# A prefix-sum mask, V without copies and a new order in the opening of an attention + FFN kernel

## The chip, the cores and the metric

The kernel runs on one core of a Trainium2 chip. The metric is the device time of one execution in microseconds; lower is better. The kernel before takes 326.36 us, the median of three runs (326.13 to 328.28).

## The reference

Causal attention in a sliding window of 64 keys over 8 batches of 8 heads, 576 tokens of 64 dimensions each, and behind it a gated FFN over all 4608 tokens. Inputs and output are float32.

```python
B, H, S, D = 8, 8, 576, 64
scores = (1.0 / np.sqrt(D)) * np.matmul(q, k.transpose(0, 1, 3, 2))
rel = pos[:, None] - pos[None, :]
scores = np.where((rel >= 0) & (rel < 64), scores, -1e9)
attn = softmax(scores)                      # over the keys
x = np.matmul(attn, v)                      # to (4608, 512), heads side by side
g = x @ w_gate                              # 512 x 1536
out = (g * sigmoid(g) * (x @ w_val)) @ w_out   # 1536 x 512
```

## The kernel before

**Tiling.** The 4608 tokens are cut into 36 chunks of 128 and 9 FFN chunks of 512. A query sees at most 64 keys back, so a chunk of 128 queries needs its own 128 keys and the last 64 of the chunk before. Matmuls take bfloat16 and accumulate in float32 in the eight PSUM banks.

**One chunk of attention.** `Sa`, `Sbias` and `Sb` make the scores of chunk n, keys on the partitions, queries along the columns. A score tile has 128 rows for 192 keys: rows 0 to 63 hold the chunk's lower 64 keys, against all 128 queries; rows 64 to 127 hold the 64 keys of the chunk before for the lower 64 queries, and the chunk's own upper 64 keys for the upper 64 queries. In the first four chunks the mask is a matmul that adds `nmask` (0 or -30000) to the bank ahead of the scores (`Sbias`, L459); later chunks multiply the exponentials by `mask` (`Sm`). ScalarE takes the exponential into `pt` (L491). The product with V has a 65th column of ones, so that each result carries its denominator; VectorE divides (`AVn`, L628 and L631) into `xb`. `X` transposes `xb` on PE (L743), and ScalarE or VectorE copies the result into `xT`.

**V in the first chunks.** Queries of the lower half need the own lower keys on partitions 0 to 63 and the keys of the chunk before on partitions 64 to 127. `shift` therefore copies halves of `va` into `vs` on POOL or ScalarE (L298, L296), and `AVs` multiplies per head once by `vs` for the lower 64 queries and once by `va` for the upper 64, each over 128 partitions (L612). Chunk 0 has no chunk before it and takes `va` alone (L609).

**The opening.** `build` writes the order of the first four chunks out by hand, with the PSUM banks in two written lists (`banks`). Each engine works through its own instructions in order, and an instruction waits by semaphore for what it reads and overwrites. k of the first 256 tokens comes through SP's and ACT's DMA queues (`first_loads`). All else comes through POOL's queue: `load2` for q and k in pairs of chunks, `load` for v, `load_w` for pieces of the gate and value weights. POOL also makes `ident` and two steps of the mask with `affine_select` (`init_ident` L320, `init_mask` L329) in the same sequence. PE runs matmuls on zeros (`warm`, L789) while k arrives and in some gaps. `Fs` makes a step of the FFN: a Wg group, then a Wv group (L818), tanh on ScalarE (L825), two products on VectorE (L827, L829). It is a generator, so `build` can place other work between its groups.

**Behind the opening.** `EARLY`, `LOADS` and `SHIPS` list the further steps, and `pump` issues loads as soon as the step that frees their buffer is recorded. At most 16 of POOL's DMAs are outstanding, since it uses 16 semaphores in turn. A bank is then picked by when the recorder's cost model has it free.

Of the kernel before, what the change touches and what calls it, by code (L numbers as in the profile page):

```python
# [7 lines left out]
ALU = mybir.AluOpType  # L8
# [12 lines left out]
F32 = dt.float32  # L21
# [145 lines left out]
class _Kernel:  # L167
# [41 lines left out]
    def alloc(self):  # L209
        nc = self.nc  # L210

        def sb(name, n, dtype=BF):
            return nc.alloc_sbuf_tensor(name, [128, n], dtype)
# [4 lines left out]
        self.ident = sb("ident", 128)  # L218
# [84 lines left out]
    def init(self):  # L303
        g = self.g
        self.zero(self.wup[:, :], ["wup"])
        g.op("act", lambda e: e.activation(self.wup[:, :], self.wup[:, :], ACTF.Exp), writes=["wup"])
        self.zero(self.wz[:, :], ["wz"])
        self.zero(self.ident[:, :], ["ident"])
        self.zero(self.mask[:, :], ["mask"], 1.0)
        self.init_va(0, 4)  # L310
        for i in range(3):
            self.zero(self.vs[i][:, :, 64:80], [("vs", i, 0), ("vs", i, 1)], 1.0)
# [9 lines left out]
            pattern=[[-1, 128]], channel_multiplier=1), writes=["ident"])  # L322

    def init_mask(self):
        g = self.g
        mm = self.mask[:, :].rearrange("p (v e q) -> p v e q", v=3, e=2)
        a, b = mm[:, :, 0, :], mm[:, :, 1, :]
        for fill, base in ((0.0, 0), (1.0, 64)):
            g.op("pool", lambda e, fill=fill, base=base: e.affine_select(  # L329
                out=a, in_=a, compare_op=ALU.is_ge, fill=fill, base=base,  # L330
                pattern=[[0, 3], [1, 64]], channel_multiplier=-1), writes=["mask"])
        src = mm[:, 0:1, 0, :].to_broadcast([128, 3, 64])
        one = g.op("dve", lambda e: e.tensor_scalar(b, src, -1.0, 1.0, ALU.mult, ALU.add), reads=["mask"], writes=["mask"])
        g.op("dve", lambda e: e.memset(mm[64:128, 1, 0, :], 0.0), writes=["mask"])
        g.op("dve", lambda e: e.memset(mm[0:64, 2, 1, :], 0.0), writes=["mask"], after=one)

    def init_nmask(self):
        self.g.op("dve", lambda e: e.tensor_scalar(
            self.nmask[:, :], self.mask[:, :], 1.0, 30000.0, ALU.subtract, ALU.mult), reads=["mask"], writes=["nmask"])

    def init_kmask(self):
        g = self.g
# [255 lines left out]
    def AVs(self, st):  # L598
        n, bx, av, done = st
        va, pt = self.va[n], self.pt[n % self.NP]  # L600
        iv = self.VS[n]
        vs = self.vs[iv] if n else va

        def pe(e):
            for j in range(4):
                for p in range(2):
                    h = 2 * j + p
                    if n == 0:
                        x = e.matmul(av[:, p, j, :], pt[:, h, :], va[:, h, 0:65], start=j == 0, stop=True, skip_group_check=True)  # L609
                        continue  # L610
                    for c, vv in ((0, vs), (1, va)):
                        x = e.matmul(av[64 * c:64 * c + 64, p, j, :], pt[:, h, 64 * c:64 * c + 64], vv[:, h, 0:65],  # L612
                                     start=j == 0, stop=True, skip_group_check=True)
# [6 lines left out]
        done.append(self.g.op("pe", pe, reads=rd, writes=[b[1] for b in bx]))  # L620

    def AVn(self, st):
        n, bx, av, _ = st
# [277 lines left out]
    def loads(self):  # L901
        self.first_loads()
        self.load2(0, "q")
        self.load2(1, "k")
        self.init()
        self.init_ident()
        self.first_cast("k", 0, "dve")
        self.init_mask()
        self.load2(1, "q")
        self.load(0, "v")  # L910
        self.load(1, "v")
        self.load(2, "v")
        self.load(3, "v")
        self.load_w("g", 0, 2)
        self.load_w("v", 0, 2)
        self.load_w("g", 2, 4)
# [5 lines left out]
        self.W(4, 6)  # L922
        self.W(6, 8)

    def ready(self, t):

# [70 lines left out]
    def main(self, t):  # L997
        w = t[0]
        if w == "F":
            c, f = t[1:].split(".")  # L1000
            h = f[-1] if f[-1] in "ab" else ""
# [16 lines left out]
        elif w in "kq":  # L1018
            n = int(t[1:-1])
# [7 lines left out]
        elif w == "A":  # L1027
            n = int(t[1:])
# [3 lines left out]
        elif w == "N":  # L1032
            n = int(t[1:])
            self.AVn(self.held[n])
            self.did.add("a%d" % n)
        elif w == "B":
            n = int(t[1:])
            self.need("v%d" % n, "v%d" % (n - 1), "s%d" % n)
            st = self.AVa(n)
# [6 lines left out]
        elif w == "P":  # L1046
            n = int(t[1:])
            self.need(*["v%d" % m for m in (n - 1, n, n + 1)], "s%d" % n, "s%d" % (n + 1))
            bx = self.two("a") + [self.bank("a")]
# [8 lines left out]
        elif w == "X":  # L1058
            n, e = t[1:].split("/")
            n = int(n)  # L1060
            self.need("a%d" % n)
            self.X(n, e.rstrip("+"), half="+" in e)
            self.did.add("x%d" % n)
        elif w == "H":
            h, e = t[1:].split("/")
            n, r, i = map(int, h.split("."))
            self.need("v%d" % n, "V")
            self.shift(n, r, e, i)
            self.did.add("h" + h)
        elif w == "D":  # L1070
            self.store()
        elif w == "V":
            self.init_va(4, self.NV)
        elif w == "K":
            self.init_kmask()
        self.did.add(t)
# [30 lines left out]
    def build(self):  # L1107
        F, S, AV, X, T2, O = self.F, self.S, self.AV, self.X, self.T2, self.O
        self.loads()
        self.banks("a", [0, 1, 2, 3, 4, 5, 6, 7, 0, 1, 4, 5, 2, 3, 0, 1, 6, 7, 4, 5, 2, 3, 0, 1, 6, 7, 2, 3])  # L1110
# [33 lines left out]
        self.AVs(a2)  # L1144
        self.AVn(a2)
        a3 = self.AVa(3)
        self.AVs(a3)
# [12 lines left out]
        next(f2, None)  # L1160
        next(f1)
        next(f1, None)
        for n in range(4):
# [54 lines left out]
```

## Time and profile before

| | before |
|---|---|
| median of three runs | 326.36 us (326.13 to 328.28) |
| profiled execution | 325.66 us |
| its span, first to last instruction | 323.9 us |
| PE / VectorE / ScalarE / POOL busy | 97 / 63 / 42 / 34% |
| first FFN matmul starts at | 15.92 us |

The profile is of one execution. The span runs from the first instruction to the last; the rest of the execution's time lies around it. A row of the timeline has a start, a length, the engine, the line in the kernel, the operation, the tile written and those read, and the count where several follow one another; in square brackets stands how long the engine had idled and what ended that. The chain of waits follows the work that ended last back to what released it, step by step.

### The profile page before, as it was taken

How to read it: one execution, taken by the hardware profiler on the slowest of the kernel's cores; microseconds unless marked ns; L12 is line 12 of the kernel's file. 1: busy time of each engine (PE TensorE's matmuls, PEld its weight loads, DVE VectorE, ACT ScalarE, POOL GpSimd, SP SyncE). 2: the span in 40 equal slices, each digit the busy share in tenths (PEclk: the TensorE clock that was granted, in tenths of full speed). 3: DMA queues.
4: the chain of work that ended last, by engine and by line, in shares of the span. 5: the costliest groups of instructions: out<-in, count | busy, mean ns of one | idle time of the engine just before them, and what ended most of it. 6: DMA issues, size and time to landing. Idle time of an engine off the chain costs nothing.

```text
span 323.9 us, 7964 instructions
## 1 busy us (share of the span) xinstructions
PE 315.4 (97%) x3395; PEld 170.3 (53%) x3430; DVE 204.1 (63%) x355; ACT 136.1 (42%) x244; POOL 109.8 (34%) x138
## 2 busy tenths in 40 slices
PE   8899999999999999999999999999999999999996
PEld 7585588855455444545454444545454544444443
DVE  5678888853657738666657575756666566555510
ACT  4735854545354335433334343525252522322322
POOL 8999990007930703315050607070502000000000
DMA  9999999999999996969699989999976202000012
GB/s 145 176 190 169 170 175 153 143 140 120 141 156 143 117 161 111 151 163 150 147 159 166 157 137 113 134 127 135 119 119 74 67 34 64 35 32 33 32 67 97
DMA packets 165412, 39.85 MB, mean 123 GB/s; under 512 B 152705, under 2 KB 160641, under 8 KB 165377
## 3 DMA queue, kind: packets, MB, share of 16 engines
q0 software_dynamic: 115152, 18.62, 82.1%
q1 hardware_dynamic: 44896, 11.22, 26.0%
q10 hardware_dynamic: 5328, 9.51, 8.1%
q8 instruction: 27, 0.44, 0.6%
q14 instruction: 9, 0.07, 0.1%
HBM read 37.75 MB, written 9.44 MB: 146 GB/s over the span
## 4 chain that ended last, share of the span: by engine, by line
PE 92%; ACT 2%; DMA 2%; issue 1%; POOL 1%; DVE 0%; POOLq 0%
PE ps L818 57%; PE ps L850 28%; PE ps L661 2%; DMA va<-in_v_dram 2%; ACT pt L491 1%; PE ps L883 1%; PE ps L516 1%; ACT pt L528 1%; PE ps L479 1%; PE ps L423 1%; PE ps L743 1%; POOL qs L381 0%; PE ps L483 0%; PE ps L612 0%; ACT vs L296 0%
## 5 line engine op out<-in xcount | busy, mean ns | idle before, releaser
L818 PE MATMUL ps<-xT,Wv 128*128 128x512 bf16 (+1 forms) x486 | 110.5, 351 | 0.5
L818 PE MATMUL ps<-xT,Wg 128*128 128x512 bf16 (+1 forms) x479 | 107.6, 351 | 2.4 <-issue 1.4
L827 DVE SCALAR_TENSOR_TENSOR uu<-sig,ps 128x512 bf16<-128x512 bf16 (+1 forms) x109 | 74.0, 679 | 56.4 <-ACT sig L825 55.7
L825 ACT ACTIVATE sig<-ps 128x512 bf16<-128x512 f32 (+1 forms) x109 | 64.9, 597 | 79.8 <-PE ps L818 78.7
L850 PE MATMUL ps<-Wo,hT 128*128 128x512 bf16 x413 | 94.7, 379 | 0.6 <-ACT pt L491 0.3
L829 DVE SCALAR_TENSOR_TENSOR hT<-uu,ps 128x512 bf16<-128x512 bf16 (+1 forms) x109 | 74.3, 682 | 3.7
L818 PEld LDWEIGHTS ps<-xT,Wv 128*128 128x128 bf16 x496 | 48.5, 98 | 44.9
L369 POOL DMA_DIRECT2D kn<-in_k_dram x31 | 29.3, 949 | 122.8 <-PE ps L850 93.5
L818 PEld LDWEIGHTS ps<-xT,Wg 128*128 128x128 bf16 x496 | 46.6, 98 | 41.4
L850 PEld LDWEIGHTS ps<-Wo,hT 128*128 128x128 bf16 x420 | 40.9, 98 | 48.7
L857 ACT ACTIVATE ost<-ps 128x512 f32<-128x512 f32 x35 | 20.9, 597 | 89.9 <-PE ps L850 83.9
L369 POOL DMA_DIRECT2D va<-in_v_dram x40 | 36.0, 955 | 12.3 <-PE ps L850 12.3
L369 POOL DMA_DIRECT2D qn<-in_q_dram x31 | 29.5, 960 | 0.0
L688 DVE RECIPROCAL rp<-ps 128x14 f32<-128x14 f32 (+1 forms) x28 | 5.7, 203 | 36.0 <-PE ps L661 36.0
L491 ACT ACTIVATE pt<-ps 128x512 bf16<-128x512 f32 x36 | 19.0, 597 | 4.4 <-PE ps L483 4.1
L690 DVE TENSOR_TENSOR xb<-ps,rp 128x896 bf16<-128x896 f32 (+1 forms) x28 | 19.4, 692 | 1.0
L528 ACT ACTIVATE pt<-ps 128x512 bf16<-128x512 f32 x36 | 18.6, 602 | 2.3 <-PE ps L520 2.1
L661 PEld LDWEIGHTS ps<-va,pt 64*64 64x64 bf16 x888 | 10.8, 107 | 6.1 <-issue 5.5
L661 PE MATMUL ps<-va,pt 64*64 64x65 bf16 x888 | 13.4, 194 | 0.1
L543 DVE TENSOR_TENSOR pt<-pt,kmask 128x1024 bf16<-128x1024 bf16 x18 | 12.3, 684 | 0.0
L543 DVE TENSOR_TENSOR pt<-pt,mask 128x1024 bf16<-128x1024 bf16 x13 | 8.7, 686 | 0.8 <-ACT pt L491 0.8
L893 DVE COPY ost<-ps 128x128 f32<-128x128 f32 x1 | 0.3, 291 | 11.8 <-PE ps L883 11.8
(72 smaller groups left out, 151.0 us busy)
## 6 DMA issues: line engine op xcount, KB each, us to landing
out_dram<-ost ACTq DMA_DIRECT2D x35, 256.0 KB, 2.1
va<-in_v_dram POOLq DMA_DIRECT2D x32, 128.0 KB, 6.2
kn<-in_k_dram POOLq DMA_DIRECT2D x25, 128.0 KB, 4.9
qn<-in_q_dram POOLq DMA_DIRECT2D x25, 128.0 KB, 5.4
Wg<-in_moe_w_gate_dram POOLq DMA_DIRECT2D x6, 256.0 KB, 7.4
Wv<-in_moe_w_val_dram POOLq DMA_DIRECT2D x6, 256.0 KB, 7.1
Wo<-in_moe_w_out_dram POOLq DMA_DIRECT2D x2, 768.0 KB, 18.2
qs<-in_q_dram POOLq DMA_DIRECT2D x3, 256.0 KB, 8.6
```

Of the source, the lines that this page charges most:

```text
L369: self.g.op("pool", lambda e, d=d, a=a: e.dma_start(d, a), writes=ks, dma=True, after=self.hold)
L491: g.op("act", lambda e, po=po, p=p: e.activation(po, sv[p], ACTF.Exp, scale=SCALE), reads=[bx[p][1]], writes=[pk[p]])
L528: g.op("act", lambda e, po=po, p=p: e.activation(po, sv[p], ACTF.Exp, scale=SCALE), reads=[bx[p][1]], writes=[pk[p]])
L543: self.g.op("dve", lambda e: e.tensor_tensor(pt, pt, m, ALU.mult), reads=pk + [key], writes=pk)
L661: z = e.matmul(self.psa[64 * c:64 * c + 64, o:o + 65], pt[p][rows, h, 64 * a:64 * a + 64], va[m][rows, h, 0:65], start=first, stop=phase = ...
L690: g.op("dve", lambda e, d=d, num=num, rb=rb: e.tensor_tensor(d, num, rb, ALU.mult), reads=bk + [("rp", k)], writes=xk, cost=(1.0, 0.25)[k])
L818: r = e.matmul(bank[:, a * n:a * n + n], W[:, kk, f * 128:f * 128 + 128], xT[:, kk, lo:hi], start=(kk == 0), stop=(kk == NK - 1))
L825: g.op("act", lambda e, G=bank: e.activation(sig[:, 0:w], G[:, 0:w], ACTF.Tanh, scale=0.5), reads=[bk], writes=[("sig", i)])
L827: g.op("dve", lambda e: e.scalar_tensor_tensor(uu[:, 0:w], sig[:, 0:w], 1.0, G[:, 0:w], ALU.add, ALU.mult), reads=[("sig", i), gk], writes ...
L829: g.op("dve", lambda e: e.scalar_tensor_tensor(out, v3(uu), 0.5, v3(V), ALU.mult, ALU.mult), reads=[("uu", i), vk], writes=[("hT", ih, f) ...
L850: r = e.matmul(OB[:, :], hT[:, f, 128 * u:128 * u + 128], self.Wo[:, f, :], start=(f == 0), stop=(f == NF - 1), skip_group_check=mid is no ...
L857: g.op("act", lambda e: e.activation(ost[:, :], OB[:, :], ACTF.Copy), reads=[ok], writes=[("ost", io)])
```

## The change

The mask of one 128x128 tile is made by VectorE as a running sum along each row: from the identity matrix and the same matrix shifted by 64 columns, beginning with 0 in the upper and 1 in the lower rows. `nmask` now has two variants and is made right after it; the other variants of `mask` are made later (`init_masks`, with token `V`). POOL's sequence loses the mask steps and the four copies, and `ident` moves ahead of the load of k of the second pair. ScalarE's two copies of V go too. A new `AVh` takes the place of `AVs` for chunks 1 to 3: the lower 64 queries read both chunks' `va` where they lie, in two passes of half height, and the upper 64 queries use all 128 partitions. The fillers change in number and place, and so do the order of bias, scores, transposes and FFN groups and the list of banks.

```diff
+        self.id3 = sb("ident", 192)
+        self.ident = self.id3[:, 0:128]
+        self.edge = sb("edge", 1, F32)
-        self.nmask = sb("nmask", 3 * 128)
+        self.nmask = sb("nmask", 2 * 128)
...
     def init_mask(self):
         g = self.g
+        g.op("dve", lambda e: e.tensor_copy(self.id3[:, 128:192], self.id3[:, 0:64]), reads=["ident"], writes=["id3"])
+        g.op("dve", lambda e: e.tensor_tensor_scan(
+            self.mask[:, 0:128], self.id3[:, 0:128], self.id3[:, 64:192], self.edge[:, 0:1], ALU.add, ALU.subtract),
+            reads=["ident", "id3", ("edge", 0), ("edge", 1)], writes=["mask"])
+
+    def init_masks(self):
         mm = self.mask[:, :].rearrange("p (v e q) -> p v e q", v=3, e=2)
-        for fill, base in ((0.0, 0), (1.0, 64)):
-            g.op("pool", lambda e, fill=fill, base=base: e.affine_select(
...
+        one = self.g.op("dve", lambda e: e.tensor_copy(out, two), reads=["mask"], writes=["mask"])
+        one = self.g.op("dve", lambda e: e.memset(mm[64:128, 1, 0, :], 0.0), writes=["mask"], after=one)
+        self.g.op("dve", lambda e: e.memset(mm[0:64, 2, 1, :], 0.0), writes=["mask"], after=one)
...
+    def AVh(self, st):
+        n, bx, av, done = st
+        va, vb, pt = self.va[n], self.va[n - 1], self.pt[n % self.NP]
+
+        def half(e, phase):
+            for j in range(4):
+                for r in range(2):
+                    p = r ^ phase
+                    h = 2 * j + p
+                    rows = slice(64 * r, 64 * r + 64)
+                    x = e.matmul(av[0:64, p, j, :], pt[rows, h, 0:64], (va, vb)[r][rows, h, 0:65],
+                                 start=phase == 0 and j == 0, stop=phase == 1, skip_group_check=True)
+            return x
+
+        def full(e):
+            for j in range(4):
+                for p in range(2):
+                    h = 2 * j + p
+                    x = e.matmul(av[64:128, p, j, :], pt[:, h, 64:128], va[:, h, 0:65], start=j == 0, stop=True, skip_group_check=True)
+            return x
...
+        one = self.g.op("pe", lambda e: half(e, 0), reads=rd, writes=bk)
+        self.g.op("pe", full, reads=rd, writes=bk)
+        done.append(self.g.op("pe", lambda e: half(e, 1), reads=rd, writes=bk, after=one))
...
         self.load2(0, "q")
-        self.load2(1, "k")
         self.init()
         self.init_ident()
+        self.load2(1, "k")
+        self.load2(1, "q")
+        self.init_mask()
+        self.init_nmask()
         self.first_cast("k", 0, "dve")
-        self.init_mask()
-        self.load2(1, "q")
...
-        self.shift(0, 1, "pool")
-        self.shift(1, 1, "pool")
-        self.load_w("v", 2, 4)
-        self.shift(2, 1, "pool")
-        self.shift(3, 0, "pool")
+        for n in range(4):
+            self.load(n, "v")
+        for f in range(0, 8, 2):
+            self.W(f, f + 2)
...
-        self.warm(84, n=58)
+        self.warm(72, n=68)
         self.first_cast("k", 1, "act")
-        self.init_nmask()
...
         self.Sb(s0)
-        self.warm(3, j=0)
         T2(1, "k", ("dve", "dve"))
         self.Sb(s1)
+        self.warm(2, j=4)
         T2(1, "q", ("dve", "act"))
         self.start()
+        s2 = self.Sa(2, True)
         a0 = self.AVa(0)
         self.AVs(a0)
-        self.shift(1, 0, "act")
         self.AVn(a0)
-        s2 = self.Sa(2, True)
         self.Sb(s2)
-        self.shift(2, 0, "act")
         a1 = self.AVa(1)
-        self.AVs(a1)
+        self.AVh(a1)
...
         f0 = self.Fs(0, (0, 1), 0, 256)
         next(f0)
-        next(f0)
         X(2, "act", "a")
         X(3, "dve", "a")
+        next(f0)
         next(f0, None)
-        f1 = self.Fs(0, (2, 3), 0, 256)
-        next(f1)
         f2 = self.Fs(0, (0, 1), 256, 512)
         next(f2)
         next(f2)
         next(f2, None)
+        f1 = self.Fs(0, (2, 3), 0, 256)
+        next(f1)
         next(f1)
         next(f1, None)
```

Behind the opening the engines' instructions stand in the same order as before, but for `init_masks` on VectorE.

More of the change, by code (lines that the diff above doesn't have):

```diff
@@ L308, in init @@
         self.zero(self.ident[:, :], ["ident"])
-        self.zero(self.mask[:, :], ["mask"], 1.0)
+        self.zero(self.edge[0:64, :], [("edge", 0)])
+        self.zero(self.edge[64:128, :], [("edge", 1)], 1.0)
         self.init_va(0, 4)
@@ L325, in init_mask @@
         g = self.g
[L326 to L335 removed]
+        g.op("dve", lambda e: e.tensor_copy(self.id3[:, 128:192], self.id3[:, 0:64]), reads=["ident"], writes=["id3"])
[3 more added lines that the diff above has]
+    def init_masks(self):
+        mm = self.mask[:, :].rearrange("p (v e q) -> p v e q", v=3, e=2)
+        two = self.mask[:, 0:128].unsqueeze(1).to_broadcast([128, 2, 128])
+        out = self.mask[:, 128:384].rearrange("p (v x) -> p v x", v=2)
+        one = self.g.op("dve", lambda e: e.tensor_copy(out, two), reads=["mask"], writes=["mask"])
+        one = self.g.op("dve", lambda e: e.memset(mm[64:128, 1, 0, :], 0.0), writes=["mask"], after=one)
+        self.g.op("dve", lambda e: e.memset(mm[0:64, 2, 1, :], 0.0), writes=["mask"], after=one)
     def init_nmask(self):
[L338 to L339 removed]
+        two = self.mask[:, 0:128].unsqueeze(1).to_broadcast([128, 2, 128])
+        out = self.nmask[:, :].rearrange("p (v x) -> p v x", v=2)
+        one = self.g.op("dve", lambda e: e.tensor_scalar(out, two, 1.0, 30000.0, ALU.subtract, ALU.mult), reads=["mask"], writes=["nmask"])
+        self.g.op("dve", lambda e: e.memset(self.nmask[64:128, 128:192], -30000.0), writes=["nmask"], after=one)
     def init_kmask(self):
@@ L1073, in main @@
             self.init_va(4, self.NV)
+            self.init_masks()
         elif w == "K":
@@ L1143, in build @@
         a2 = self.AVa(2)
-        self.AVs(a2)
+        self.AVh(a2)
         self.AVn(a2)
         a3 = self.AVa(3)
-        self.AVs(a3)
+        self.AVh(a3)
         self.AVn(a3)
```

15 lines of the change are left out of this document (4 added, 11 removed).

## The prediction

> **What bounds the kernel now.** I read the page first, then what PE waits for after the opening, then the chain of waits over the first 19 us.
>
> ```profile
> span 323.9 us, 7964 instructions
> PE 315.4 (97%) x3395; PEld 170.3 (53%) x3430; DVE 204.1 (63%) x355; ACT 136.1 (42%) x244; POOL 109.8 (34%) x138
> ...
> q8 instruction: 27, 0.44, 0.6%
> ```
>
> PE is busy for 97% of the span. What it waits for from 16 us to the end is one short list (engine, line and waited for; us in total, times, longest):
>
> ```profile
> PE ps L818 <- issue: 1.4, 9, 0.2
> PE ps L818 <- ACT pt L528: 0.5, 3, 0.2
> ...
> ```
>
> These make 1.9 us in 308, the rows below them 0.3 each, and none is on work that the change touches. So behind the opening the kernel is bound by PE, and a microsecond won or lost in the opening comes out at the end one for one. The question is only when PE gets through the opening. The chain of waits there (start, length, what):
>
> ```profile
> 2.33 0.88 POOL ks L381
> ...
> 3.29 0.32 POOL ident L320
> ...
> 4.50 0.91 POOL qs L381
> 5.41 0.86 POOL va L369
> 6.27 6.03 DMA va<-in_v_dram
> ...
> 12.32 0.63 ACT vs L296
> ...
> 13.93 0.51 ACT vs L296
> ...
> 15.54 0.44 PE ps L612 x14
> ```
>
> V of chunk 1 lands at 12.30, ScalarE shifts it, and two scores with their exponentials follow until the last attention product (15.54). Both ACT copies that the change removes are in this chain, and POOL's issues of q and V stand at its head. Whether those issues really set the landing is the first thing to settle. Bytes moved in three stretches (us, busy time of each engine, clock, DMA share, GB/s), the issues with their time to landing, and POOL's issues of the first weights:
>
> ```profile
> 4.00:8.50 4.50, 4.35 (x78) 3.21 (x76) 2.62 (x7) 1.82 (x3) 4.35 (x6) 1.00 1.65 174
> 8.50:12.00 3.50, 2.92 (x82) 1.89 (x71) 1.97 (x3) 2.66 (x5) 3.14 (x5) 1.00 2.29 153
> 13.50:23.00 9.50, 9.24 (x135) 7.75 (x134) 7.15 (x15) 4.54 (x9) 9.46 (x14) 1.00 1.46 197
> ...
> qs<-in_q_dram POOLq DMA_DIRECT2D x1, 256.0 KB, 6.1
> va<-in_v_dram POOLq DMA_DIRECT2D x4, 128.0 KB, 6.0
> Wg<-in_moe_w_gate_dram POOLq DMA_DIRECT2D x1, 256.0 KB, 6.5
> Wv<-in_moe_w_val_dram POOLq DMA_DIRECT2D x1, 256.0 KB, 7.1
> ...
> 8.87 0.80 POOL L387 DMA_DIRECT2D Wg<-in_moe_w_gate_dram  x1
> 9.62 0.79 POOL L387 DMA_DIRECT2D Wv<-in_moe_w_val_dram  x1
> ```
>
> The queue moves 174, 153 and 197 GB/s without a hole. V's landings (5.41 + 6.0 = 11.4, then 6.27 + 6.03 = 12.3) lie 0.86 us apart, which is what 128 KB take at 153 GB/s; the weights (8.87 + 6.5 = 15.4, 9.62 + 7.1 = 16.7) lie 1.35 apart, which is 256 KB at 197. So the queue is drained as fast as it goes. The change keeps the order of these transfers (q0, k1, q1, V0 to V3, then Wg and Wv in turn), so I leave every landing where it is, although POOL issues q1 at about 2.33 + 0.4 for ident + 0.88 for k1 = 3.6 instead of 4.50, and V 0.9 us earlier with it. The Trainium skill (DMA: Bandwidth & Descriptors, Anatomy of one DMA) puts one such transfer at about 2 us fixed plus bytes over 436 GB/s; an estimate from that page is 2.3 us for 128 KB against the 6.0 measured, so by that rule most of the 6.0 is time in a full queue, which the even 153 GB/s bear out.
>
> **The change part by part.** The stretch of PE and VectorE that it rewrites:
>
> ```profile
> 5.99 0.59 PE L459 MATMUL ps<-nmask,ident 128*128 128x512 bf16 x2
> ...
> 10.64 0.64 PE L426 MATMUL ps<-ident,qs 128*64 128x128 bf16 x16 [0.27 <-DMA qs<-in_q_dram]
> 11.59 0.40 PE L609 MATMUL ps<-va,pt 128*128 128x65 bf16 x8 [0.31 <-DMA va<-in_v_dram]
> 13.01 0.22 PE L612 MATMUL ps<-vs,pt 128*64 128x65 bf16 x1 [0.20 <-ACT vs L296]
> ...
> 13.38 0.60 PE L459 MATMUL ps<-nmask,ident 128*128 128x512 bf16 x2
> ...
> 14.29 0.62 PE L743 MATMUL ps<-ident,xb 128*128 128x128 bf16 x8
> 14.84 0.22 PE L612 MATMUL ps<-vs,pt 128*64 128x65 bf16 x1
> ...
> 15.92 1.05 PE L818 MATMUL ps<-xT,Wg 128*128 128x256 bf16 x8
> ...
> 17.67 0.61 PE L743 MATMUL ps<-ident,xb 128*128 128x128 bf16 x8
> 18.15 1.92 PE L818 MATMUL ps<-xT,Wg 128*128 128x256 bf16 x16
> ...
> 4.09 0.60 DVE L298 CAST ost<-hT 128x512 bf16<-128x512 f32 x1 [1.39 <-DMA hT<-in_k_dram]
> 5.12 0.34 DVE L338 TENSOR_SCALAR nmask<-mask 128x384 bf16<-128x384 bf16 x1
> ...
> 13.73 0.69 DVE L631 TENSOR_TENSOR xb<-ps,rc 128x512 bf16<-128x512 f32 x1
> ...
> 15.40 0.20 DVE L628 RECIPROCAL rc<-ps 128x8 f32<-128x8 f32 x1
> ...
> 16.47 0.69 DVE L631 TENSOR_TENSOR xb<-ps,rc 128x512 bf16<-128x512 f32 x1
> ```
>
> *Mask.* The copy, scan, nmask and memset go into VectorE's 1.39 us of idling before the cast at 4.09. No scan is in this trace; its bounds are the 0.20 us of a reciprocal and four times the 0.34 us of a 128x384 op, and I take 0.3 (128 elements are nearest to the 0.34 row, with a third of its width). POOL's select of ident (0.32) now starts where k1's issue did (2.33), so ident is ready near 2.7, the four end by about 3.6, and the cast keeps its start: cost zero. Nor does it win anything, since bias 0 never waited for nmask in this trace: nmask ends at 5.46, bias 0 comes at 5.99, right behind the transposes.
>
> *Fillers.* 72 of 68 columns stand for 84 of 58: 4896 columns against 4872, zero. The three 512-column fillers behind score 0 go, two come behind score 1; PE waits for q1 there (4.50 + 6.1 = 10.6, transposes 10.64) in either order, so zero.
>
> *Chunk 1.* Without the copy its products need V1 alone. AV0 started some 0.13 us after its V landed (11.59 against 11.4 to 11.5), so chunk 1 starts at 12.43 instead of 13.01: 0.58 won. Bias 2, AV0 and score 2, which stand ahead of it, need q1's transposes and V0, and the vs copy no longer stands between score 2 and its exponentials.
>
> *Price of AVh.* L612 issues 16 matmuls, and the next instruction comes 0.37 us after the first. AVh issues 8 half-height, 8 full-height and 8 half-height ones; a full one costs 0.03 us (L609: 8 in 0.40 with some 0.19 of drain), 8 halves about 0.10. The second halves wait for the first, and the full ones between cover that if it takes 0.25 or less. I take 0.57 to the next instruction, 0.20 more than now; the bounds are no loss and 0.45 more, if nothing covers that wait.
>
> *The sum to the FFN.* Bias 3 comes at 13.00 instead of 13.38. From bias 3 to the last product nothing changes (13.38 to 15.54: 2.16), so AV3 starts at 15.16, and with its own 0.20 more the first Wg group at 15.74 instead of 15.92. Its weights (15.4) and the copies of xT are there. The transposes between hold nothing up: X1 is asked for at 14.29 less 0.38 and half of the pair's 0.5, near 14.15, and xb1 (now 13.73 + 0.69) comes 0.38 earlier, at 14.04.
>
> *The new order behind it.* The transposes of chunks 2 and 3 now stand ahead of the first Wv group. A group of 8 takes 0.88 us (the 16 at 18.15 take 1.92 with some 0.17 of drain), four transposes 0.23 (8 in 0.61 with drain), so Wg ends at 16.62, X2 at 16.85. X3 needs xb3, the last of VectorE's chain, now done at 16.47 + 0.69 = 17.16. That chain starts when AV2's result is there: AV2 moves with bias 3, from 14.84 to 14.46; its result comes 0.49 plus the 0.20 later, at 15.15, instead of the 15.40 at which VectorE was free for it, so xb3 is done 0.25 earlier, at 16.91. X3 runs from 16.97 to 17.20, PE having idled 0.12; Wv (landed 16.7) runs to 18.08. Now the same four pieces end at 18.15. Won: 0.07 us. The six half groups behind are the same work in another order, and their weights land earlier than they are asked for.
>
> *Moved to later.* init_masks (one copy narrower than the 0.34 row, two small memsets) goes behind the memsets of token V in VectorE, at most 0.5 us. Cover: eight PSUM banks, of which a step takes two; without it, 0.5.
>
> So the sum is 0.1 us off the profiled run (325.66, its span and 1.76 around it). The three timed runs have their median at 326.36, 0.7 above the profiled one; taken off that median, the forecast is 326.3, and 325.9 to 326.8 with the bounds. The lower end is AVh at no extra price, where Wv's landing (16.7 + 0.13, and 0.88 of work to 17.7) stops the gain at 0.45; the upper end is AVh at 0.45 more, which puts Wg at 16.24 and xb3 at 17.41, and the loss is 0.43.
>
> **The rivals.** *Deliveries move with the issue.* If landings follow POOL's 0.9 us, or if an instruction fetch (q8: 27 in 0.6% of 16 engines' 324 us, about 1.15 us each on one engine) misses the engine that lands last, q1, V and weights come up to 1.0 us earlier, all steps above move with them: 325.3. For it: V's constant 6.0 from issue to landing. Against it: the even GB/s, and the weights, whose 6.5 and 7.1 grow with the queue. A brake on it stands further on: the pair of q2 transposes.
>
> ```profile
> qs<-in_q_dram POOLq DMA_DIRECT2D x1, 256.0 KB, 11.1
> ...
> 27.39 1.76 POOL L381 DMA_DIRECT2D qs<-in_q_dram  x1
> 39.15 0.45 PE ps L423 x8
> ```
>
> The q of the third pair lands at 38.5 and PE asks for it at 39.15, so a gain over 0.65 us waits here if that landing stays.
>
> *Slower: PE stands behind xb3.* X3 is ahead of Wv in PE's queue, and PE goes in order; behind it wait all FFN groups, and ACT and VectorE for these. Each 0.1 us by which VectorE ends later than 17.0 is 0.1 us of PE. It decides from 0.1 us beyond my 16.91. AV2's and AV3's second halves price it: if their wait is not covered, 326.8, and 327.0 with VectorE's copies of xT in the way by another 0.2.
>
> *Slower: POOL is held up by VectorE.* If VectorE's added copy, nmask and the cast keep POOL from writing descriptors of k1 and q1, up to their 0.1 + 0.3 + 0.6 us, V lands up to 1.0 later once the queue runs dry: 327.3. Against it: the issue at 4.50 took 0.91 beside the cast and nmask. The Trainium skill (SBUF — State Buffer, SBUF: two separate sides) has this as a rule, the "DVE blocks DMA" trap; the 0.91 speaks against it here.
>
> *The change doesn't do what it says.* A scan of over 1.2 us delays the cast; some 1.5 us more are absorbed in the fillers and in the wait for q1, then it costs one for one: at 3.5 us, ten times the 0.34 row, 327.1.
>
> **How the numbers follow.** Forecast (325.9 to 326.8) 0.60; earlier deliveries 0.17; xb3 0.15; POOL held up or the scan 0.06; something unseen 0.02. The range takes in the first three with their prices, 325.2 to 327.0. A change of 1% is 3.3 us, about what a measurement of this kernel can tell from no change; no case but the unseen and the scan reaches it: faster 0.02, same 0.95, slower 0.03.
>
> **What would show it.** Right: cast at 4.09, q1's transposes near 10.6, chunk 1 at 12.4, the next bias about 0.57 behind it, Wg near 15.7, a short idle of PE ahead of X3 put down to xb, the second pair's Wg group near 18.1. Wrong: V's first product before 11.3 (deliveries moved), the cast after 4.2 (scan), POOL issues over 1.1 us, or PE waiting for weights.

## The result: 5 us slower, and the profile after

The change takes 331.7 us (median of six, 330.1 to 333.28) against 326.61 us (six, 326.05 to 331.87) beside it: 1.0148 times before, 95% interval 1.011 to 1.0187. The forecast was 326.3, with a range of 325.2 to 327.0. Here and below, medians are of all executions, while a ratio and its interval leave out those more than 1.5% above the fastest of the same kernel, so the two can differ. The profiled execution took 330.88 us, with a span of 329.1. Its page begins so (span; busy time by engine; granted clock in 40 slices; the queue that brings instructions):

```profile
span 329.1 us, 7976 instructions
...
PE 317.4 (96%) x3405; PEld 171.5 (52%) x3441; DVE 204.9 (62%) x359; ACT 135.2 (41%) x242; POOL 106.8 (32%) x132
...
PEclk9899999999999999999999999999999999999999
...
q8 instruction: 27, 0.44, 0.6%
```

PE has hardly more instructions (3405 for 3395); its work is stretched. The granted clock is below full in the slice from 8.2 to 16.5 us. The table by stage shows it more finely (start and end, length, busy time of PE, PEld, DVE, ACT, POOL, clock, DMA share, GB/s): it was 0.50, half of full, from about 14.3 to 17.7 us (the 0.79 and 0.80 are means of half and full).

```profile
14.00:14.50 0.50, 0.50 (x14) 0.46 (x13) 0.00 (x0) 0.00 (x0) 0.50 (x2) 0.79 1.45 198
15.00:17.00 2.00, 2.00 (x34) 1.28 (x32) 0.86 (x2) 0.73 (x2) 2.00 (x4) 0.50 1.45 197
17.50:18.00 0.50, 0.50 (x14) 0.46 (x14) 0.13 (x1) 0.00 (x0) 0.50 (x2) 0.80 1.51 224
```

PE's timeline shows where the time goes, in the very stretch that the change rewrites, and at two places behind it:

```profile
11.07 0.41 PE L617 MATMUL ps<-va,pt 128*128 128x65 bf16 x8
11.66 0.19 PE L640 MATMUL ps<-va,pt 64*64 64x65 bf16 x1
...
11.69 0.26 PE L640 MATMUL ps<-va,pt 64*64 64x65 bf16 x6
11.87 0.25 PE L648 MATMUL ps<-va,pt 128*64 128x65 bf16 x2
13.97 0.35 PE L648 MATMUL ps<-va,pt 128*64 128x65 bf16 x6 [1.84 <-issue]
14.24 0.42 PE L640 MATMUL ps<-va,pt 64*64 64x65 bf16 x8
14.60 1.03 PE L467 MATMUL ps<-nmask,ident 128*128 128x512 bf16 x2
...
18.90 0.83 PE L854 MATMUL ps<-xT,Wg 128*128 128x256 bf16 x6
...
32.70 0.62 PE L431 MATMUL ps<-ident,qs 128*128 128x128 bf16 x8 [0.47 <-ACT kT L298]
...
53.45 0.27 PE L854 MATMUL ps<-xT,Wg 128*128 128x256 bf16 x1 [1.19 <-issue]
```

Chunk 1's products start 1.35 us earlier than before (11.66 against 13.01). Then PE stops between the second and the third product of one and the same group, where no semaphore stands, for 1.84 us, "issue": it waits for nothing that the profile shows. Behind it, at half the clock, the bias takes 1.03 us for 0.60. The first Wg group comes at 18.90, 2.98 later than before. Later, 0.47 us go in a wait for ScalarE's copy of k's transposes, which before did not have, and 1.19 us in a second stop without a releaser. These make 4.64 of the 5.2 us by which the span has grown; the other 0.6 were not followed.

**What stops PE.** Queue q8 carries 27 packets, 0.44 MB: 16 KB each. The records of PE and PEld are 3405 + 3441 = 6846 instructions, 254 for each packet. Counted in the program (a product, its weight load and a wait for a semaphore are one each), the first stop comes behind instruction 448 and the second behind instruction 1472, four times 256 later. So PE's program comes in blocks of 256 instructions, in packets beside those of the data, and PE stopped where a block ended. The list of DMA packets, for 8.1 to 8.4 us of before and 11.6 to 11.9 us of after, holds the first such packet of each:

```profile
q8 instruction: 1, 0.02, 22.2%
```

```profile
q8 instruction: 1, 0.02, 20.0%
```

It starts at 8.21 us before and at 11.72 after; PE goes on 2.25 us behind its start. When a block is asked for is not in the trace; only where its packet starts is.

VectorE's part went nearly as the prediction said (its timeline of after), and POOL's transfers were faster than it said (list of issues; the last number is the median time from issue to landing):

```profile
2.92 0.48 DVE L331 TENSOR_TENSOR_SCAN mask<-ident,edge 128x128 bf16<-128x128 bf16 x1
...
4.13 0.50 DVE L300 CAST ost<-hT 128x512 bf16<-128x512 f32 x1 [0.29 <-DMA hT<-in_k_dram]
```

```profile
va<-in_v_dram POOLq DMA_DIRECT2D x4, 128.0 KB, 5.6
...
qs<-in_q_dram POOLq DMA_DIRECT2D x1, 256.0 KB, 5.6
```

q1 is issued at 3.48 instead of 4.50 and lands at 9.07 instead of 10.60; V0 at 9.91 instead of 11.46.

### The profile page after: what moved, and what is told of

The parts are those of the page before. It is cut to its first block, busy times and chain, and to the rows that moved or that the text cites. A ratio compares the mean times of both kernels' runs of the same rounds, so it can differ in the third digit from the quotient of the medians.

```text
span 329.1 us, 7976 instructions
## 1 busy us (share of the span) xinstructions
PE 317.4 (96%) x3405; PEld 171.5 (52%) x3441; DVE 204.9 (62%) x359; ACT 135.2 (41%) x242; POOL 106.8 (32%) x132
## 4 chain that ended last, share of the span: by engine, by line
PE 94%; issue 2%; ACT 2%; DMA 1%; DVE 0%
PE ps L854 57%; PE ps L886 27%; PE ps L697 2%; DMA hT<-in_k_dram 1%; PE ps L487 1%; PE ps L779 1%; PE ps L919 1%; PE ps L524 1%; PE ps L467 1%; ACT pt L499 1%; ACT pt L536 1%; PE ps L491 1%; PE ps L434 1%; PE ps L431 1%; PE ps L640 0%
## 5 line engine op out<-in xcount | busy, mean ns | idle before, releaser
L929 DVE COPY ost<-ps 128x128 f32<-128x128 f32 x1 | 0.3, 292 | 11.8 <-PE ps L919 11.8
```

## The experiments

The first theory, FETCH: the block is asked for when PE has passed a certain number of instructions. With 72 fillers for 84 that comes later, when POOL's transfers already fill the DMA engines, and AVh without copies brings PE to the block's end sooner. Rivals: the two passes hold PE up by themselves (AVH), or POOL's earlier issues do it whatever the fillers (QUEUE).

### The number of fillers

```diff
-        self.warm(72, n=68)
+        self.warm(84, n=58)      # 24 columns fewer in all; further runs: 150 of 32, 100 of 49
```

> Edit: the changed kernel with 84 fillers of 58 columns again (24 PE instructions more ahead of the first transposes, same duration), nothing else. Theory FETCH: PE ran dry at its 449th instruction because the block of 256 instructions behind it was asked for behind q0's transposes (about 7 us) instead of during the fillers (before 5.3 us), and so stood behind V in the DMA engines. Expects the instruction packet near 8.2 us, no idle time of PE over 0.3 us put down to issue between 6 and 30 us, q1 landing near 10.5 again, the first Wg group at 15.4 to 15.9, and 325.5 to 327.0 us. Rival QUEUE: PE is starved because POOL now issues V and the weights without a pause, whatever the fillers. Expects the stall of 1.5 to 2 us in chunk 1 to stay, Wg near 18.9, 331 us. Rival AVH: the two passes of half height hold PE up by themselves. Expects the same as QUEUE, 331 us.

327.6 us, 1.0041 [1.0007, 1.0074]. The packet lies at 9.96, later than the 8.2 expected, and there is no stop. Four of the five microseconds are back, with 24 columns of filler fewer. The packet now hits V0, which lands at 12.02, and the first Wg group comes at 16.63; that and the time lie above what I expected. The same kernel was timed once more, beside the change itself:

> The change with 84 fillers once more, timed beside the change itself. FETCH: asked for 12 fillers earlier, the block comes in time in nearly every execution: median 327.2 to 327.8, narrower than the change's, and 2 to 4 us under it where the change's executions run dry. If the fillers' number means nothing: the same median as the change.

327.55 us, 1.0041 [1.0025, 1.0057], where the change had 330.97. What is left, 1.3 us, is taken up further below.

> Edit: the changed kernel with 150 fillers of 32 columns, so that the first block is asked for at about 3 us, when POOL's queue is nearly empty. FETCH: its packet starts before 6.5 us and does not stand in V's way, q1 lands near 9.1 and V of chunk 1 near 10.8 as in the changed kernel; no stall in chunk 1. But all block ends move: the next one, instruction 705, now falls in the V products of chunks 2 and 3, and its block is asked for near 9.5 us in a full queue, so a stall of 0 to 2 us there, Wg at 14.7 to 17 us, 325.2 to 328 us. QUEUE and AVH: stall in chunk 1 as in the changed kernel, 331 us.

> Edit: the changed kernel with 100 fillers of 49 columns. FETCH: the block is asked for some 0.5 us earlier than with 84, its packet starts between 6.5 and 8.3 us, no stall in chunk 1; instruction 705 lies in the first FFN groups, which PE works through more slowly than the attention, so no stall or one under 0.5 us; 325.2 to 326.8 us. QUEUE and AVH: stall in chunk 1, 331 us.

331.18 us, 1.0081 [1.003, 1.0131], and 328.89 us, 1.0071 [1.0026, 1.0115]. The first block comes early as expected (packets at 5.51 and 7.16), but the next one is then due in the opening as well. PE runs dry at instruction 705, which is 449 + 256, in other work each time: with 150 fillers in AVh of chunk 2, with 100 in the first Wg group, behind packets at 13.39 and 15.27. One row of each timeline, and for 150 fillers a second:

```profile
15.87 0.28 PE L640 MATMUL ps<-va,pt 64*64 64x65 bf16 x6 [0.94 <-issue]
...
107.50 0.25 PE L697 MATMUL ps<-va,pt 64*64 64x65 bf16 x5 [2.09 <-issue]
```

```profile
17.78 0.72 PE L854 MATMUL ps<-xT,Wg 128*128 128x256 bf16 x5 [1.57 <-issue]
```

The stop at 107.50 comes ten blocks of 256 behind the first, as far as the records let one count, and ends 2.51 us behind a packet at 104.99. Both times lie above my expectation, and with 100 fillers I had expected no stop of over 0.5 us. So more fillers are no remedy either; 84 lies between two losses.

Before with 72 fillers:

> Edit: the kernel before with 72 fillers of 68 columns, nothing else of the change. FETCH: the block is asked for near 7 us here too, its packet starts between 10.5 and 12 us, PE idles 0.8 to 2.5 us put down to issue at its 449th instruction (in the V product of chunk 1), and the time is 327.5 to 331 us. QUEUE: POOL still pauses at its copies, so no stall, 326.4 us within 0.5. AVH: not in this kernel, so no stall, 326.4 us within 0.5.

> Before with 72 fillers once more, one look: where does the packet lie, which came at 9.74 us the first time and at 12.36 in the change with a pause of POOL, although both have 72 fillers and issue q1 and V at the same times. CHANCE (the place in the queue differs from execution to execution): another place, by over 0.5 us, and a time off by as much or more. KERNEL (something in the change moves the request): 9.5 to 10 again.

327.44 us, 1.0012 [0.9968, 1.0056], then 326.66 in one execution. No stop of PE over 0.4 us without a releaser, against my expectation. The packet came at 9.74 and at 11.63: its place differs from one execution to the next. At 11.63 it delayed PE only from 13.64 to 13.99, since there PE waits for V and ScalarE's copy and reaches its 449th instruction 1.7 us later than in the change. The fillers alone don't lose 5 us; they need a PE that comes early. The first profile shows another way to be slow, at 330.44 us: q1 lands at 11.99, PE waits 1.36 us for it, and near 71 us it waits 2.05 for a later piece of V, with the clock at half for some 3.4 us behind that. So a time of 330 alone doesn't prove a late block.

### The place of the stop

```diff
-        self.warm(2, j=0)
+        self.warm(14, n=73, j=0)     # behind the first q's transposes: 24 instructions more
```

> The change with its 72 fillers, and the two fillers of 512 columns behind the transposes of the first q replaced by fourteen of 73 columns: the same time on PE, but 24 instructions more behind the place where the block is asked for and ahead of the place where it ran out. FETCH (blocks of 256 instructions, counted from the start of PE's program): the packet comes near 11.7 us again, PE runs dry 12 products earlier, in the last products of score 2 or at AVh's very first, not between its second and third full-height product, idles 2 to 2.5 us on issue there, and starts again some 2.25 us behind the packet's start, near 14.0. AVH (the two passes hold PE up): it idles at the same product of AVh as in the change, 1.84 us.

329.78 us. The packet starts at 11.07, and PE stops twelve products earlier, among the last of score 2, for 1.45 us where I expected 2 to 2.5; AVh, behind it, runs through:

```profile
11.65 0.20 PE L491 MATMUL ps<-qT,kT 64*64 64x64 bf16 x2
13.30 0.22 PE L491 MATMUL ps<-qT,kT 64*64 64x64 bf16 x2 [1.45 <-issue]
13.30 0.31 PE L640 MATMUL ps<-va,pt 64*64 64x65 bf16 x8
```

That is the block's end, moved by exactly the 24 instructions. One block on, PE stops once more, for 0.41 us at 19.55, 2.53 behind a packet at 17.02. AVH falls.

### The queue ahead of the packet

A pause of POOL puts q1 and V back to their old issue times:

```diff
         self.load2(1, "k")
+        self.pause()                  # two selects on a spare tile, 0.9 us
         self.load2(1, "q")
```

> The change with 72 fillers, and POOL held up for 0.9 us between k1 and q1 as before (two selects on a spare tile), so that q1 and V are issued no earlier than before. FETCH (the block is asked for at the same place of PE as in the change, near 6.7 us, and waits behind what POOL has put in the queue by then): the queue is 0.9 us shallower, the packet comes near 10 to 11 us instead of 11.72, and V lands later, so PE reaches the end of its block at 12.4 or later: idle on issue there 0 to 0.7 us instead of 1.84, no stretch at a clock under 1.0, first Wg 16.6 to 17.2, time 327.6 to 328.5. FILLERS ALONE (the 72 fillers make the stall whatever POOL does): 1.84 us of idling again, 331. Rival on the remainder: what is left over before is the price of AVh, 3 times 0.43, and 0.47 for the bank of the third pair's q.

330.34 us, 1.0055 [1.0014, 1.0096]. Missed: the packet lies at 12.36, and PE stops at the same product for 1.97 us:

```profile
14.81 0.35 PE L657 MATMUL ps<-va,pt 128*64 128x65 bf16 x6 [1.97 <-issue]
```

So QUEUE as put at first falls too: the stop doesn't need POOL's lead of 0.9 us. How often it comes with the pause one profile can't say; the ten executions spread from 326.92 to 333.64. V held back altogether:

```diff
         T2(0, "q", ("act", "dve"))
+        self.rest()                   # V0 to V3 and the weights, held until these transposes are done
```

> The change with its 72 fillers, and POOL's issues of V0 to V3 and of the first weights held back until PE has done the transposes of the first q (near 7.3 us), so that only q1 is still under way when the block is asked for. QUEUE (the block's packet stands behind what POOL has handed to the DMA engines before it): the packet starts at 9.3 at the latest, when q1 is through, 2 us earlier than in the change (11.72) and in the pause run (12.36); PE gets its block by 11.6, ahead of V1, which is issued near 8.2 and lands near 13, so there is no idling on issue in AVh of chunk 1. FIXED DELAY (the block takes some 5 us from its request, whatever stands in the queue): the packet at 11 to 12.4 again.

330.03 us; PE now waits 0.63 us for V and 0.85 for Wv, and the rest was not followed. The packet starts at 8.58, while q1's last pieces land, and PE passes the place without a stop:

```profile
12.72 0.31 PE L640 MATMUL ps<-va,pt 64*64 64x65 bf16 x8 [0.63 <-DMA va<-in_v_dram]
12.96 0.44 PE L648 MATMUL ps<-va,pt 128*64 128x65 bf16 x8
```

With the V transfers out of the way the block comes 3.1 us earlier than in the change's first profile, and 1.2 earlier than in any other with 72 fillers (9.74 to 12.36). FIXED DELAY falls; QUEUE, in the sense of this run, is borne out by one execution: the packet waits behind POOL's data. The packets with 84 fillers agree: 8.21 and 7.27 in before and in the run "The price of AVh", which have POOL's old order, and 9.4 to 10.0 with the change's. The mask part alone is one of these (excerpt; the later `init_nmask` goes):

```diff
-        self.load2(1, "k")
         self.init()
         self.init_ident()
-        self.first_cast("k", 0, "dve")
-        self.init_mask()
+        self.load2(1, "k")
         self.load2(1, "q")
+        self.init_mask()
+        self.init_nmask()
+        self.first_cast("k", 0, "dve")
```

> Before, with the change's mask alone (prefix sum, nmask and masks as in the change, POOL's issues in its order), V's copies, AVs, 84 fillers and the written order as before. Earlier issue moves the landings of q1, V0 and V1 up by 0.9 us but for the packet, which comes near 9.5 to 10 and hits V0 or V1: V1 near 12.0 to 12.4, first Wg at 15.6 to 15.95, no idling on issue. The cost model then takes bank 2 for the third pair's q: 0.47 us of waiting for kT near 30 us. Time 326.5 to 327.0. If the masks themselves cost (VectorE late for the first cast), Wg after 16.2 and 327.3 or more.

326.61 us, 1.001 [0.9971, 1.0049]. With 84 fillers and POOL's earlier issues the packet lies at 9.68 (8.21 before), q1 lands at 9.53, V0, hit by the packet, at 11.82, and the first Wg group comes at 16.18. The 0.47 us of waiting for kT are there. A gain or loss of the mask by itself can't be told.

### The change again

> The change once more, one look, unchanged. The packet at 11.0 to 12.4, as in the three runs with 72 fillers in the change's order, and 1.4 to 2 us of idling on issue between the second and third full-height product of chunk 1, because PE comes to that place before the block whatever the execution. Open is what else belongs to the change and what to one execution: CLOCK (the clock under 1.0 behind the idling: 0.89 in the change's profile, 1.0 in two runs that idled as long) and SECOND (the idling of 1.2 us at 52 us, not there in the pause run, whose PE program is as long). Each that shows again belongs to the change more often than not; the time then near 331, without both near 328.5.

> The change, unchanged, timed again beside the other runs of this call. The look before had the block's packet at 9.77 us instead of 11.72, no idling on issue, and 326.74 us. CHANCE OF THE EXECUTION (the packet's place differs from one execution to the next): times between 326.5 and 333.5 within this call, in two groups or a wide spread, the median 2 us or more above before's. CHANCE OF THE CALL (chip or session set it, the same for all executions of a call): all within 1 us of each other, either near 326.8 or near 331.

> The change, one more profiled execution on the same chip as the timed runs. Packet after 11 us: idling on issue in AVh of chunk 1 of 1.4 to 2 us and a time of 329 or more. Packet before 10.5: no idling there, 326.7 to 327.5.

326.74 us, then 330.97 (five executions, 329.85 to 332.55; 1.0138 [1.011, 1.0167]), then 326.81 on the same chip. Of thirteen executions of the change eleven took 329.85 to 333.28 and two took 326.7 to 326.8, with none between. The first time is against my expectation. The profiles tell why they differ. In the two good ones the packet starts at 9.77 and 9.78 (list of packets, 9.7 to 10.0 us, and PE's timeline of the last one):

```profile
q8 instruction: 1, 0.02, 20.0%
```

```profile
12.19 0.31 PE L640 MATMUL ps<-va,pt 64*64 64x65 bf16 x8 [0.47 <-DMA va<-in_v_dram]
12.43 0.44 PE L648 MATMUL ps<-va,pt 128*64 128x65 bf16 x8
12.80 0.31 PE L640 MATMUL ps<-va,pt 64*64 64x65 bf16 x8
13.05 0.60 PE L467 MATMUL ps<-nmask,ident 128*128 128x512 bf16 x2
...
16.10 1.05 PE L854 MATMUL ps<-xT,Wg 128*128 128x256 bf16 x8
```

In the timed one it starts at 11.77, and everything is as in the first profile:

```profile
14.28 0.35 PE L648 MATMUL ps<-va,pt 128*64 128x65 bf16 x6 [2.01 <-issue]
```

```profile
13.00:14.50 1.50, 0.22 (x6) 0.22 (x5) 0.00 (x0) 0.13 (x1) 1.50 (x4) 1.00 1.46 195
15.00:17.00 2.00, 2.00 (x32) 1.12 (x31) 0.86 (x2) 0.47 (x1) 2.00 (x4) 0.50 1.45 197
```

The half clock and a second stop near 52 us (1.0 us this time) go with the late packet in both of these profiles; in the two good executions there is neither. Up to the first Wg group the late execution loses 2.80 us to a good one (18.90 against 16.10). The stop's 1.84 and at most 1.7 for the 3.4 us at half the clock, less the 0.53 by which chunk 1 started earlier (11.66 against 12.19), make 3.0 at most. Only two of the eleven long executions were profiled; that the other nine lose their time the same way is likely, not shown. What puts the packet at 9.8 or at 11.7 with 72 fillers stays open. Both good executions were taken singly and the eleven others in series, but the single execution with the block's end moved had its packet at 11.07 all the same. With 84 it lay between 9.4 and 10.0 in all seven profiles that have the change's order of POOL.

### The price of AVh

```diff
-        self.AVs(a1)                  # and a2, a3; POOL's copies and all else as before
+        self.AVh(a1)
-        self.shift(1, 0, "act")
-        self.shift(2, 0, "act")
```

> Before, with AVh for chunks 1 to 3 in place of AVs, and without ScalarE's two copies; POOL's sequence, its four copies (now read by nobody), fillers and order as before. PRICE (24 products of AVh take 0.80 us against 0.37 of AVs, as the run with 84 fillers has them): 0.58 won at chunk 1, 3 times 0.43 lost, first Wg at 16.6, time 0.7 over before. As predicted (0.20 each, 0.18 won): first Wg at 15.74, time 0.2 under before. No idling on issue over 0.3 in either.

326.94 us, 1.0033 [1.0001, 1.0065]; first Wg at 16.84; PRICE holds. AVh takes 0.86 us to the next instruction in chunk 1 where AVs took 0.37 (the rows from 12.19 to 13.05 above show its parts: 0.24 + 0.37 + 0.25), and from chunk 1's first product to the first Wg group there are 3.91 us instead of 2.91. I had set eight half-height products at 0.10, and they do follow each other at that pace: in the change's profile they start from 11.66 to 11.76 (the six from 11.69 take 0.26, one alone 0.19). But the first full one starts at 11.87, 0.11 behind the last of them, where products of one kind follow at 0.03 to 0.05. What costs is going from one kind to the other.

Can the full ones run beside the halves?

```diff
                     x = e.matmul(av[0:64, p, j, :], pt[rows, h, 0:64], ...
+                if phase == 0:
+                    x = upper(e, j, 0)        # one full-height product behind every two halves
```

> As the run with banks 4 and 5, and in AVh half of the full-height products are woven between the first half-height ones (two halves, one full, four times), then the other four, then the second halves. COLUMNS (half-height products of the lower queries all use the same half of PE's columns and follow each other at 0.03 us, full ones of the upper queries use the other half and could run beside them): AVh takes 0.65 to 0.7 instead of 0.80, first Wg 0.3 to 0.45 earlier, time 326.7. NO OVERLAP: 24 products take 0.80 in any order, time 327.1; if the second halves' wait for the first shows, 0.1 more each, 327.4.

331.11 us, 1.0128 [1.0058, 1.0198]; AVh now takes 1.56 us (4 executions). Its beginning:

```profile
12.07 0.22 PE L648 MATMUL ps<-va,pt 64*64 64x65 bf16 x2
12.22 0.22 PE L640 MATMUL ps<-va,pt 128*64 128x65 bf16 x1
12.37 0.22 PE L648 MATMUL ps<-va,pt 64*64 64x65 bf16 x2
```

Across each change between 64 and 128 rows there are 0.15 us from start to start, where products of one kind follow each other at 0.03 to 0.05. COLUMNS falls, the other way round, and so does NO OVERLAP, which had 0.80 in any order. The Trainium skill (TensorEngine Tiling (Array Packing), Key Properties) says that a change of tiling mode drains TensorE; the 0.15 agree.

### The bank

```diff
+            if (st, x) == (2, "q"):           # third pair's q: banks 4 and 5, as before
+                self.free.remove(4 + cc)
+                bank, bk = self.ps[4 + cc], ("ps", 4 + cc)
```

> The change with 84 fillers, and the transposes of the third pair's q written to banks 4 and 5, as before, instead of bank 2, which k's transpose has just filled. BANK: PE's 0.47 us of waiting for ScalarE's copy kT near 30.7 us goes, and the time falls by 0.5 from 327.6 to 327.1. LATE SCALARE (ScalarE is late there anyway): PE waits as long a step further on, time 327.6.

The wait is gone: q's transposes follow k's at once.

```profile
29.04 0.61 PE L435 MATMUL ps<-ident,ks 128*128 128x128 bf16 x8
29.48 0.61 PE L435 MATMUL ps<-ident,qs 128*128 128x128 bf16 x8
```

The times don't show it: 328.27 us (326.33 to 332.11), 1.0043 [1.0019, 1.0067], inconclusive for half a microsecond. The recorder's figures tell where the wait came from: in before its cost model had bank 4 free ahead of bank 2 and took it; with the mask part, alone or in the change, it has bank 2 free 0.2 us ahead of bank 4, and puts q where k's transposes stand whose copy is still to come.

### What is left of the change

```diff
         # 84 fillers, banks 4 and 5, AVh for chunk 1
-        self.AVh(a2)                  # and a3
+        self.AVs(a2)                  # with three copies on POOL, one on ScalarE
```

> The change with 84 fillers, banks 4 and 5 for the third pair's q, and AVh for chunk 1 alone; chunks 2 and 3 have AVs and their four copies (three on POOL, one on ScalarE) as before. PRICE: 2 times 0.43 us of the two passes go, first Wg near 15.1, and PE then waits for Wv at most 0.2 us; the profiled execution 0.7 to 0.9 under the run with banks 4 and 5, near 326.0, a median near 327.4 or less. COPIES (the copies hold POOL or ScalarE up): first Wg at 15.6 or later, and as slow as the run with banks 4 and 5.

> The change with 84 fillers, banks 4 and 5 for the third pair's q, and AVh for chunk 1 alone, timed once more for a narrower interval against before: 0.9988 [0.9954, 1.0023] the first time. EVEN: 0.998 to 1.002 again, no gain that can be told. GAIN: 0.997 or less with an interval wholly under 1, if its profiled 324.9 us of span is not typical.

326.8 us, 0.9988 [0.9954, 1.0023], then 326.18 us, 1.0003 [0.9983, 1.0023]: even with before. Chunk 1 starts at 12.23 and the first Wg group at 15.62 (timeline of the second run; 15.1 was expected of this kernel), 3.39 us for 2.91 before and 3.91 with three AVh:

```profile
12.23 0.31 PE L644 MATMUL ps<-va,pt 64*64 64x65 bf16 x8
...
15.62 1.05 PE L858 MATMUL ps<-xT,Wg 128*128 128x256 bf16 x8
```

Two AVh less save 0.43 each, but from chunk 1 to the first Wg group that is only 0.52, since chunk 3 then waits 0.25 for its exponentials. Between the profiled executions of this kernel and of the change with 84 fillers the first Wg group comes 0.33 earlier (15.62 against 15.95); with the bank's 0.47 that makes 0.80, and the spans differ by 0.8 (324.4 and 325.2). The medians differ by 1.37, and the other half microsecond was not followed. So the loss of the change has three parts: instructions that come late, with what follows from that (3.4 to 4.1 us between the medians with 84 and with 72 fillers); AVh in chunks 2 and 3; and the bank. The shares of the last two are read from the traces, not from times.

## Why the prediction was wrong, point by point

- *Fillers* is the step that failed: "4896 columns against 4872, zero". The columns are nearly equal; the number of instructions isn't, and with it moves the place of the next block's packet: in the change's order of POOL it lay at 9.8 to 11.8 with 72 fillers, at 9.4 to 10.0 with 84, at 7.16 with 100 and at 5.51 with 150. In place of the zero the runs showed a stop of 1.84 us and 3.4 to 4.1 us between the medians. Of the instruction fetch I had priced only which transfer it hits, not that PE can run out of instructions. The Trainium skill (Runtime: NRT & Kernel Launch, Instruction fetch mechanics) describes the blocks of 256 instructions in 16 KiB and calls the cost of crossing one mostly hidden; the 27 packets agree with the first, the 1.84 us speak against the second.
- *What bounds the kernel now*: "I leave every landing where it is" failed. The 0.86 us between V's landings, which I read as the queue's rate, are also the distance of POOL's issues, so they could not tell a full queue from one that follows its issuer. q1 landed 1.5 us earlier in the change and 1.1 earlier with the mask alone (10.60 to 9.53), and AV0 started at 11.07, before the 11.3 that I had set as the sign of it. The first rival had this right and its price with the wrong sign: the earlier data stand ahead of the block.
- *Mask*: right for VectorE. The scan took 0.48 us for my 0.3, within its bounds, and the cast came at 4.13 for 4.09.
- *Chunk 1*: without the copy it could start with V1: 11.66, or 12.19 where the packet hits V1, for my 12.43.
- *Price of AVh*: mis-sized, 0.43 to 0.49 for 0.20, beyond the upper bound in chunk 1 and near it in chunks 2 and 3. The halves' own 0.10 was right; what the sum left out is the change between 64 and 128 rows, 0.11 to 0.15 us each time.
- *The sum to the FFN*: 16.06 and 16.10 in the executions without a stop, for 15.74; 18.90 and 19.21 with it.
- *The new order behind it*: right. From the first Wg to the first Wv group 1.44 us in the good execution with 16.10 (17.54), for 1.46 worked out; no wait for xb3, so the second rival did not happen.
- *Moved to later*: hidden in time, but not in the plan: with the mask part the recorder's bank pick changes, 0.47 us.
- *Slower: POOL is held up*: did not happen, its issues of k1 and q1 took 0.91 each. The scan was not slow.
- "a microsecond won or lost in the opening comes out at the end one for one": not borne out so closely. In the good executions the first Wg group is 0.14 to 0.18 late and the bank costs 0.47, but the spans are 1.0 to 1.1 longer than before's; with AVh for chunk 1 alone the group is 0.30 early and the span 0.5 longer. Single executions don't settle half a microsecond.

The range to 327.0 holds the two executions in thirteen in which the block came in time, at 326.7 and 326.8. Even there the sum is not right: AVh costs more, and the bank was not in it.

## What to carry to other kernels

Count instructions, not only columns and microseconds: PE's program arrives in DMA packets beside the data, and a change that removes fillers, adds small products or fills the DMA queue earlier moves the place where PE can run dry. Idle time put down to "issue" in the middle of a group, with nothing to wait for, is the sign, where it lasts a microsecond or two; the distance between two such places, counted in instructions, and the packets of the instruction queue confirm it. Equal spacing of landings proves a full queue only if the issues are spaced otherwise, and a planner's choices have to be compared after any edit ahead of them.

## What the runs showed of the hardware

- From the start of an instruction packet to PE's next product it took 2.2 to 2.5 us where PE had run dry in the opening (11.72 to 13.97, 11.07 to 13.30, 12.36 to 14.81, 11.77 to 14.28, 13.39 to 15.87, 15.27 to 17.78), and 3.5 and 3.3 at the change's second stops (49.97 to 53.45, 50.33 to 53.59).
- With 72 fillers the packet lay near 9.8 or at 11.1 to 12.4, and in the change itself at both 9.8 and 11.7; in its four profiles the time followed it, 326.7 and 326.8 against 330.9 and 331.0.
- After a stop of 1.84 us the granted clock was 0.50 from about 14.3 to 17.7 us, after one of 2.01 from 14.7 to 18.1, and after a wait of 2.05 for V (before with 72 fillers) from 71.2 to 74.6; after stops of 1.97 (pause), 1.45 (block's end moved) and 2.09 us (150 fillers) it stayed at 1.0. What decides this was not tried.
- Across a change of PE's row tiling between 64 and 128 rows 0.11 to 0.15 us pass from start to start, so that weaving the two kinds made AVh 0.7 us longer.
